# Zero matmuls ahead of five waits of TensorE in a fused attention, routing and expert kernel

## The chip, the cores and the metric

The kernel runs on one core of one Trainium2 chip. A core has five engines that run beside each other and meet through semaphores: TensorE (PE in the rows; PEld is its weight load) multiplies matrices into PSUM, VectorE (DVE) and ScalarE (ACT) work element by element, GpSimd (POOL) does the same more slowly and issues gathers and scatters, and SyncE (SP) issues most of the transfers. PSUM has eight banks here, of 128 partitions by 2 KB. The metric is the device time of one execution in microseconds (us), the median of several runs.

## The reference, cut to what matters

```python
for t in range(S):                      # 2 batches, 8 heads, 768 steps, head size 40
    m_new = maximum(f[t] + m, i[t])
    f_stab, i_stab = exp(f[t] + m - m_new), exp(i[t] - m_new)
    C = f_stab * C + i_stab * outer(v[t], k[t]);  n = f_stab * n + i_stab * k[t]
    y[t] = sigmoid(o[t]) * (C @ q[t]) / maximum(abs(n @ q[t]), 1)
x = y.reshape(1536, 320)
noisy = x @ w_gate + log1p(exp(x @ w_noise)) * noise
# the 2 largest of 8 experts per row, softmax over the two
out = sum over the row's two experts of  weight * (relu(x @ w1[e]) @ w2[e])
# second layer: all 4 experts for every row, weighted by domain_probs
out2 = sum over e of p[:, e] * (relu(out @ v1[e]) @ v2[e])
```

## The kernel before, in words

The recurrence is computed in chunks of 128 time steps, 6 per batch, so 12 chunks i = 0 to 11 (0 to 5 are batch 0). For a chunk, `o_S(i, g)` (L338) multiplies keys and queries of four heads into a bank `sp`, for g = 0 and 1; `o_M` (L345) multiplies that by the decay mask `A` on VectorE; the mask comes from exponentials on ScalarE (`o_decay`, L327) and a triangle select on GpSimd. `o_U`, `o_Cg` and `o_Cu` carry the state `C` from chunk to chunk (GpSimd scales it by `gb`, VectorE adds the bank `up`). `o_inter` (L391) and `o_AV` (L402) fill the bank `hp`; ScalarE copies it to `hs`; `o_tp` turns it; `o_x` (L418) normalises and gates it on VectorE and so writes the chunk's rows of `x`. `o_xp` (L434) transposes these, `o_lp` and `o_lt` make the routing logits from them.

When chunks 0 to 3, then 0 to 5, have logits, `route(b, h)` (L478) ranks the experts on VectorE, counts ranks with ones-matmuls into the bank `pp` and computes a row number `slot` for each token. GpSimd then scatters the token numbers into the table `Td` in memory, eight scatters for h = 0 and four for h = 1, and `tok` is read back from it. With `tok`, GpSimd gathers the rows of the first expert unit (`xload`); `prep` transposes and splits them into a high and a low part (`xh`, `xl`), and `moe1(0)` (L638) begins with bank `s1`. From there on matmuls of the experts follow each other, with the rest of batch 1's attention and routing woven in. In parallel SyncE streams weights (`raw`), which ScalarE and VectorE split into a high and a low part (`w1hi`, `w1lo`, `w2hi`, `w2lo`).

What sets the order: the written order is that of the software pipeline `STEP` (L47), of the strings `PLAN1` and `PLAN2`, and of `weave`. On top of it the language's scheduler places the instructions of each engine by when it estimates their inputs ready, so that an instruction can stand behind others that were written after it. Each engine then executes its list strictly in that order, and waits where an input is missing. PSUM tiles take the eight banks in turn, in the order in which they are written in the program. At the start of the program there are already 11 matmuls of zeros (`WARM`).

Of the kernel before, what the change touches and what calls it, by code (L numbers as in the profile page):

```python
# [16 lines left out]
P = 128  # L17
# [15 lines left out]
LEAD = 6  # L33
PARTS = [slice(0, 1), slice(1, 2), slice(2, 4), slice(4, NC)]
WARM = 11
PLAN1 = "AAAAAAAAAAAzAAoAAAArrwArAwArrrrrArArrrrwrAAArrrArArrAwrrArArAArrrrArrrArA"
PLAN2 = "A AA  AA r A AAA r rr rr A  A AA Ar ArrrrrrrrrA Arr r  A rrrr   rr rrrrr rr  r Arr rArr r  r "
RAW = 3 * F // NQ
# [27 lines left out]
def body(ctx: ExitStack, tc: tile.TileContext, d, o, dbg=None):  # L66
    nc = tc.nc
# [10 lines left out]
    def psum(shape, name):  # L78
        uid[0] += 1
        return ps.tile(shape, F32, tag="ps", name=f"{name}_{uid[0]}")  # L80


    zero = at.tile([P, 4 * P], BF16, name="zero")
# [95 lines left out]
    def w_next(n, k, q):  # L179

        assert STREAM[pos[1]][1:] == (n, k, q)
        w_split()
        w_load()
# [5 lines left out]
    def stage1(out_ps, w1, f, xh, xl):  # L189
        hi, lo = weights[w1, 1, f // (NF // NQ)]  # L190
        c = slice((f % (NF // NQ)) * P, (f % (NF // NQ) + 1) * P)
        seq = [(hi[:, 0, c], xh[:, 0]), (hi[:, 0, c], xl[:, 0]), (hi[:, 1, c], xh[:, 1]), (hi[:, 1, c], xl[:, 1]), (lo[:, 0, c], xh[:, 0]), (lo[:, 1, c], xh[:, 1]), (hi[:, 2, c], xh[:, 2]), (lo[:, 2, c], xh[:, 2])]
        for i, (l, r) in enumerate(seq):
            nc.tensor.matmul(out_ps, l, r, start=(i == 0), stop=(i == len(seq) - 1))  # L194
# [15 lines left out]
    def relu_split(hh, hl, src):  # L210
        nc.scalar.activation(hh, src, AF.Relu)  # L211
        nc.vector.scalar_tensor_tensor(hl, src, 0.0, hh.bitcast(F32), ALU.max, ALU.subtract)  # L212
# [114 lines left out]
    def o_decay(i, g):  # L327
# [7 lines left out]
        nc.gpsimd.affine_select(A[:, hs_], A[:, hs_], pattern=[[0, 4], [1, P]], compare_op=ALU.is_ge, fill=0.0, base=0, channel_multiplier=-1)  # L335
        t["d", g] = last.ins

    def o_S(i, g):  # L338
        t = st[i]
        sp = psum([P, 4, P], "sp")  # L340
        for j in range(4):
            nc.tensor.matmul(sp[:, j, :], t["kp"][:, 4 * g + j, :], t["qt"][:, j, :], start=True, stop=True)  # L342
        t["sp", g] = sp
# [90 lines left out]
    def o_xp(i):  # L434
        b, c = divmod(i, NC)
        xp = psum([P, 3, P], "xp")
        for k in range(2):
            nc.tensor.transpose(xp[:, k, :], xs[b][:, c, k * P : (k + 1) * P], ident)
        nc.tensor.transpose(xp[0:DR, 2, :], xs[b][:, c, 2 * P : DM], ident)
        xt = at2.tile([P, 3, P], F32, name="xt")  # L440
        nc.scalar.copy(xt[:, 0:2], xp[:, 0:2])
        nc.vector.tensor_copy(xt[0:DR, 2], xp[0:DR, 2])
        st[i]["xt"] = xt
# [34 lines left out]
    def route(b, h):  # L478
# [7 lines left out]
        n = HALVES[h]  # L486
# [3 lines left out]
        sp = at.tile([P, HC, E1], F32, name=f"spl{h}")  # L490
# [15 lines left out]
        for k in range(2):  # L506
            nc.vector.tensor_scalar(sel[:, k, n], rk, float(k), None, ALU.is_equal)
        yield
        pp = psum([P, HC, E1], "pp")
        nc.tensor.matmul(pp, tri, selb[:, n], start=True, stop=False)  # L510
        last = c0 + HC - 1
        for i in range(1, last + 1):
            j = max(i, c0)
# [3 lines left out]
        g = at.tile([P, HC, E1], F32, name=f"g{h}")  # L517
# [67 lines left out]
    def tiles(n):  # L585

        return [P] * (CAP // P) if len(UNITS[n][1]) == 1 else [min(P, JCAP - i) for i in range(0, JCAP, P)]

    def xload(n):
        if n >= len(UNITS) or n in xes or n in preps or not routed.issuperset(UNITS[n][1]):  # L590
            return
        e, bs = UNITS[n]
        col = 0 if bs[0] == 0 else CAP // P
        first = n < ALONE
        X = (Xall[:NC] if first else Xall).rearrange("t p c -> (t p) c")
        xe = m1.tile([P, len(tiles(n)) if first else NCOL, DM], F32, name="xe")
        for s, r in enumerate(tiles(n)):
            nc.gpsimd.indirect_dma_start(out=xe[:r, s, :], out_offset=None, in_=X, in_offset=bass.IndirectOffsetOnAxis(ap=tok[bs[-1]][:r, e, col + s : col + s + 1], axis=0))
        xes[n] = xe

    def prep(n):
        if n >= len(UNITS):
            return
        xe = xes.pop(n)
        N = sum(tiles(n))
        pa = psum([P, 2, N], "pa") if 2 * N <= 512 else None
        pk = [pa[:, k] if pa is not None else psum([P, N], "pa") for k in range(2)]
        pb = psum([DR, N], "pb")
        for s, r in enumerate(tiles(n)):
            c = slice(s * P, s * P + r)  # L610
            for k in range(2):
                nc.tensor.transpose(pk[k][:, c], xe[:r, s, k * P : (k + 1) * P], ident[:r, :r])
            nc.tensor.transpose(pb[:, c], xe[:r, s, 2 * P :], ident[:r, :r])
        W = CAP if n < ALONE else JCAP
        xh = m1.tile([P, 3, W], F32R, name="xh")[:, :, :N]
        xl = m1.tile([P, 2, W], F32R, name="xl")[:, :, :N]
        if pa is not None:
            split(xh[:, 0:2], xl, pa)
        else:
            for k in range(2):  # L620
                split(xh[:, k], xl[:, k], pk[k])
        nc.scalar.copy(xh[0:DR, 2], pb)
        nc.vector.tensor_sub(xh[DR:P, 2], pb, xh[0:DR, 2].bitcast(F32))
        preps[n] = xh, xl
# [9 lines left out]
    def flush():  # L634
        while ystore:
            ystore.pop()()

    def moe1(n):  # L638

        e, bs = UNITS[n]  # L640
        w = wn[n]
        ahead = n + 1 == len(UNITS) or wn[n + 1] != w
        xh, xl = preps.pop(n)
        for j in (n + 1, n + 2):
            xload(j)
        ts = tiles(n)
        N = sum(ts)
        W = CAP if n < ALONE else JCAP
        hh, hl, both = [], [], []
        half = len(ts) - 1 if ts[-1] < P else None  # L650
        M = (N - ts[-1]) if half is not None else N
        for f in range(0, NF, 2):

            hf = m1.tile([P, 2, 2 * W], F32R, name="hh", bufs=5)
            hhf, hlf, htf = hf[:, :, :N], hf[:, :, 2 * N - M : 2 * N], hf[:, :, N : 2 * N - M]
            pair = psum([P, 2, N], "s1") if 2 * N <= 512 else None
            for i in range(2):
                hp = pair[:, i] if pair is not None else psum([P, N], "s1")
                stage1(hp, w, f + i, xh, xl)
                if pair is None:  # L660
                    nc.scalar.activation(hhf[:, i], hp, AF.Relu)
                    for l, c in ((hlf, slice(0, M)), (htf, slice(M, N))):
                        nc.vector.scalar_tensor_tensor(l[:, i], hp[:, c], 0.0, hhf[:, i, c].bitcast(F32), ALU.max, ALU.subtract)
                hh.append(hhf[:, i])
                hl.append(hlf[:, i])
                both.append(hf[:, i, M : 2 * N - M])
            if pair is not None:
                relu_split(hhf, hlf, pair)
            if f == 2:
                flush()  # L670
            if n == 0 or wn[n - 1] != w:
                w_next(w, 2, f // 2)
            yield
        if n + 1 in xes:
            prep(n + 1)
        yps = [psum([P, DM], "s2") for _ in ts]
        for q in range(NQ):
            stage2(yps, w, hh, hl, q, half=half, both=both)
            if ahead:
                w_next(w + 1, 1, q)  # L680
            if q < NQ - 1:
                yield
        ys = m1.tile([P, len(ts) if n < ALONE else NCOL, DM], F32, name="ys", bufs=2 if n < ALONE else 1)
        for s, r in enumerate(ts):
            if r == P:
                nc.vector.tensor_copy(ys[:, s], yps[s])
            else:
                nc.scalar.copy(ys[:r, s], yps[s][r:])
                nc.vector.tensor_add(ys[:r, s], yps[s][:r], ys[:r, s])
        row = first_row(e, bs[0])  # L690

        def store():
            k = sum(r == P for r in ts)
            nc.sync.dma_start(Yd[row : row + k * P].rearrange("(s p) c -> p s c", p=P), ys[:, :k])
            if k < len(ts):
                nc.sync.dma_start(Yd[row + k * P : row + N], ys[: ts[k], k])

        ystore.append(store)
        if n in (len(UNITS) - 1, LAST0):
            flush()  # L700
        yield
# [145 lines left out]
    def og_load(b):  # L847
        nc.sync.dma_start(xs[b], d["og"][b])

    if WARM:  # L850
        wps = psum([P, 4 * P], "warm")
        for i in range(WARM):
            nc.tensor.matmul(wps, zero[:, :P], zero, start=(i == 0), stop=(i == WARM - 1))
    og_load(0)
# [69 lines left out]
    W0 = splits()  # L924
    for w in PLAN1:
        if w in "zo":
# [123 lines left out]
```

## Time and profile before

| | us |
|---|---|
| median of 3 runs | 710.69 |
| lowest and highest | 710.33, 712.83 |
| the profiled execution | 708.15 |
| its span, first to last instruction | 706.1 |
| TensorE busy in the span | 680.1 (96%) |
| VectorE, ScalarE, GpSimd busy | 369.3, 262.1, 126.1 |
| mean granted clock of TensorE | 0.976 |

Times inside the program are counted from the start of the span. The profiled execution is 2.05 us longer than its span and 2.54 us shorter than the median. [...] A square bracket at the end of a row of the timeline is the time for which the engine stood idle before that group, and what ended it. Busy times of a matmul group run to a modelled end and overlap the next group's start.

### The profile page before, as it was taken

How to read it: one execution, taken by the hardware profiler on the slowest of the kernel's cores; microseconds unless marked ns; L12 is line 12 of the kernel's file. 1: busy time of each engine (PE TensorE's matmuls, PEld its weight loads, DVE VectorE, ACT ScalarE, POOL GpSimd, SP SyncE). 2: the span in 40 equal slices, each digit the busy share in tenths (PEclk: the TensorE clock that was granted, in tenths of full speed). 3: DMA queues.
4: the chain of work that ended last, by engine and by line, in shares of the span. 5: the costliest groups of instructions: out<-in, count | busy, mean ns of one | idle time of the engine just before them, and what ended most of it. 6: DMA issues, size and time to landing. Idle time of an engine off the chain costs nothing.

```text
span 706.1 us, 11386 instructions
## 1 busy us (share of the span) xinstructions
PE 680.1 (96%) x4427; PEld 622.7 (88%) x4427; DVE 369.3 (52%) x787; ACT 262.1 (37%) x501; POOL 126.1 (18%) x183
## 2 busy tenths in 40 slices
PE   9898688999999999999999999999999999999997
PEld 6776577999899999999889899898898998989987
DVE  7868587877565664658756334412444224332141
ACT  5558446763453543545541223302233113121120
POOL 5544572142612101124023000000000000000000
PEclk9998779999999999999999999999999999999999
DMA  6889647665665444567662003100130001001011
GB/s 195 220 246 302 196 115 234 194 202 168 172 195 163 136 135 148 135 189 244 187 189 75 1 19 109 38 1 1 31 103 31 1 1 37 1 1 39 1 37 41
DMA packets 39946, 80.03 MB, mean 113 GB/s; under 512 B 9377, under 2 KB 16465, under 8 KB 39889
## 3 DMA queue, kind: packets, MB, share of 16 engines
q1 hardware_dynamic: 36496, 70.39, 33.2%
q0 software_dynamic: 3392, 8.86, 4.5%
q8 instruction: 37, 0.61, 0.4%
q14 instruction: 21, 0.16, 0.1%
HBM read 70.20 MB, written 9.04 MB: 112 GB/s over the span
## 4 chain that ended last, share of the span: by engine, by line
PE 79%; DMA 10%; DVE 5%; issue 2%; ACT 1%; POOL 1%; SPq 0%; ACTq 0%; DVEq 0%; POOLq 0%
PE z L194 25%; PE z L208 24%; PE s L194 12%; PE s L208 10%; DMA raw<-w 4%; DMA A<-LFd 2%; PE sp L342 1%; PE s L204 1%; DMA raw<-v 1%; DMA Td<-toki,slot 1%; DMA kp<-kT 1%; DVE w2lo L175 1%; PE lp L449 1%; PE hp L407 1%; POOL Td L540 1%
## 5 line engine op out<-in xcount | busy, mean ns | idle before, releaser
L211 ACT ACTIVATE hh<-z 128x512 fp32r<-128x512 f32 x96 | 57.1, 600 | 192.4 <-PE z L194 192.3
L208 PE MATMUL z<-w2hi,hh 128*128 128x320 f32 x384 | 118.6, 309 | 0.0
L208 PE MATMUL z<-w2hi,hl 128*128 128x320 f32 x384 | 118.3, 308 | 0.0
L208 PE MATMUL z<-w2lo,hh 128*128 128x320 f32 x384 | 118.3, 308 | 0.0
L194 PE MATMUL z<-x2h,w1hi 128*128 128x512 f32 x288 | 112.4, 390 | 0.0
L208 PE MATMUL s<-w2hi,hh 128*128 128x320 f32 x448 | 107.6, 312 | 1.7 <-ACT hh L211 0.9
L212 DVE SCALAR_TENSOR_TENSOR hl<-z,hh 128x512 fp32r<-128x512 f32 x96 | 65.8, 690 | 82.5 <-ACT hh L211 82.5
L194 PE MATMUL z<-x2h,w1lo 128*128 128x512 f32 x288 | 96.6, 389 | 0.0
L194 PE MATMUL s<-xh,w1hi 128*128 128x256 f32 (+1 forms) x288 | 84.5, 312 | 3.3 <-ACT xh L186 3.3
L175 DVE TENSOR_TENSOR w2lo<-raw,w2hi 128x640 fp32r<-128x640 f32 x60 | 49.6, 828 | 65.6 <-ACT w2hi L174 65.5
L208 PEld LDWEIGHTS s<-w2hi,hh 128*128 128x128 f32 x448 | 76.7, 188 | 2.8 <-ACT hh L211 1.2
L174 ACT CAST w2hi<-raw 128x640 fp32r<-128x640 f32 x60 | 43.5, 728 | 87.2 <-PE s L204 25.3
L194 PE MATMUL z<-x2l,w1hi 128*128 128x512 f32 x192 | 74.8, 390 | 0.0
L175 DVE TENSOR_TENSOR w1lo<-raw,w1hi 128x768 fp32r<-128x768 f32 x60 | 57.2, 957 | 29.8 <-ACT w1hi L174 29.2
L208 PEld LDWEIGHTS z<-w2lo,hh 128*128 128x128 f32 x384 | 72.1, 188 | 0.6
L208 PEld LDWEIGHTS z<-w2hi,hh 128*128 128x128 f32 x384 | 72.1, 188 | 0.5
L208 PEld LDWEIGHTS z<-w2hi,hl 128*128 128x128 f32 x384 | 72.1, 188 | 0.0
L194 PE MATMUL s<-xh,w1lo 128*128 128x256 f32 (+1 forms) x288 | 70.5, 309 | 0.0
L208 PE MATMUL s<-w2lo,hh 128*128 128x320 f32 x224 | 69.2, 309 | 0.0
L194 PEld LDWEIGHTS z<-x2h,w1lo 128*128 128x128 f32 x288 | 54.1, 188 | 11.3
L174 ACT CAST w1hi<-raw 128x768 fp32r<-128x768 f32 x60 | 49.9, 836 | 36.7 <-PE s L194 15.3
L194 PEld LDWEIGHTS z<-x2h,w1hi 128*128 128x128 f32 x288 | 54.0, 188 | 10.8
(188 smaller groups left out, 1025.0 us busy)
## 6 DMA issues: line engine op xcount, KB each, us to landing
raw<-w SPq DMA_DIRECT2D x44, 384.0 KB
raw<-w SPq DMA_DIRECT2D x44, 320.0 KB
raw<-v SPq DMA_DIRECT2D x16, 384.0 KB
A<-LFd SPq DMA_DIRECT2D x10, 512.0 KB
raw<-v SPq DMA_DIRECT2D x16, 320.0 KB
kv<-kv SPq DMA_DIRECT2D x12, 324.0 KB
Yd<-ys SPq DMA_DIRECT2D x8, 320.0 KB
qt<-qT SPq DMA_DIRECT2D x12, 208.0 KB
```

Of the source, the lines that this page charges most:

```text
L174: nc.scalar.copy(hi, raw)
L175: nc.vector.tensor_sub(lo, raw, hi.bitcast(F32))
L194: nc.tensor.matmul(out_ps, l, r, start=(i == 0), stop=(i == len(seq) - 1))
L204: nc.tensor.matmul(yp, both[f], r[:, k], start=(f == 0 and i == 0), stop=(f == NF - 1 and i == 1))
L208: nc.tensor.matmul(yp, l, r, start=(f == 0 and i == 0), stop=(f == NF - 1 and i == 2))
L211: nc.scalar.activation(hh, src, AF.Relu)
L212: nc.vector.scalar_tensor_tensor(hl, src, 0.0, hh.bitcast(F32), ALU.max, ALU.subtract)
L342: nc.tensor.matmul(sp[:, j, :], t["kp"][:, 4 * g + j, :], t["qt"][:, j, :], start=True, stop=True)
L407: nc.tensor.matmul(hp[64 * j : 64 * j + 41, p, :], t["kv"][:, 4 * j + p, D:], t["A"][:, 4 * j + p, :], start=False, stop=(p == 3))
L449: nc.tensor.matmul(lp[32 * k : 32 * k + 32], wgn[r, k, :], st[i]["xt"][r, k, :], start=True, stop=True)
L540: s = nc.gpsimd.indirect_dma_start(out=Td, out_offset=bass.IndirectOffsetOnAxis(ap=slot[b][:, k, c : c + 1], axis=0), in_=toki[:, b * NC + ...
```

## The change

Five places get matmuls of a zero tile, written ahead of the instructions that would wait, into the same bank, which those instructions begin anew with `start=True`. So the values in the bank are not changed by them. The zero tile exists already. The places are the scores of chunk 7 and of chunk 9 (g = 0), the transposes `xp` of chunks 6 and 7, the rank count of `route(0, 1)` and the first bank of `moe1(0)`. Of these the rank count gets a bank of its own, `fl`, so every later PSUM tile takes the next bank in turn. In all there are 8 + 3 + 8 + 18 + 5 + 8 = 50 matmuls: 24 of 512 columns and 26 of 384.

```diff
+FILL_S = {(7, 0): 8, (9, 0): 3}
+FILL_X = {6: 8, 7: 18}
...
+    def fill(out, n):
+        for _ in range(n):
+            nc.tensor.matmul(out, zero[:, :P], zero[:, : out.shape[-1]], start=True, stop=True)
...
         sp = psum([P, 4, P], "sp")
+        if (i, g) in FILL_S:
+            fill(sp.rearrange("p j l -> p (j l)"), FILL_S[i, g])
...
         xp = psum([P, 3, P], "xp")
+        if i in FILL_X:
+            fill(xp.rearrange("p k l -> p (k l)"), FILL_X[i])
...
+        if (b, h) == (0, 1):
+            fill(psum([P, 4 * P], "fl"), 5)
         pp = psum([P, HC, E1], "pp")
...
             pair = psum([P, 2, N], "s1") if 2 * N <= 512 else None
+            if n == f == 0:
+                fill(pair.rearrange("p i c -> p (i c)"), 8)
```

The scheduler counts the new matmuls as work of TensorE, and so the order around them moves on every engine. On TensorE, before, around the scores of chunk 7 (`sp_915` is g = 0, `sp_1000` g = 1; `up_896` and `hp_977` belong to chunk 6, `lp_920` to chunk 4, `tp_955` and `xp_1005` to chunk 5):

```order
L376 MATMUL up_896<-kv,kw 40x41 x8
L342 MATMUL sp_915<-qt,kp_164 128x128 x4
L449 MATMUL lp_920<-xt,wgn 32x128 x3
...
L415 MATMUL tp_955<-ident,hs 128x105 x4
...
L342 MATMUL sp_1000<-qt,kp_164 128x128 x4
L407 MATMUL hp_977<-A,kv 41x128 x8
L438 MATMUL xp_1005<-ident,x_85 128x128 x2
```

and in the changed kernel (`sp_915` again g = 0 and now `sp_1008` g = 1, `hp_985` chunk 6, `xp_1013` chunk 5):

```order
L386 MATMUL up_896<-kv,kw 40x41 x8
...
L344 MATMUL sp_915<-zero 128x512
...
L461 MATMUL lp_928<-xt,wgn 32x128 x3
...
L425 MATMUL tp_963<-ident,hs 128x105 x4
...
L417 MATMUL hp_985<-A,kv 41x128 x8
L352 MATMUL sp_915<-qt,kp_164 128x128 x4
L352 MATMUL sp_1008<-qt,kp_164 128x128 x4
L450 MATMUL xp_1013<-ident,x_85 128x128 x2
```

The zeros stand where the scores stood, and the scores themselves have moved behind the logits of chunk 4, the rank count, and the last products of chunk 6. On ScalarE, before, from the sigmoid of batch 1's gate (`x_86`) on:

```order
L272 ACTIVATE x_86<-x_86 128x1920
L451 COPY ls<-lp_920 96x128
L333 ACT_TABLE_LOAD
L333 ACTIVATE A<-A,as_t 128x128 x8
L441 COPY xt<-xp_1005 128x256
L409 COPY hs<-hp_977 105x512
L174 CAST w1hi<-raw 128x768 x3
```

and in the changed kernel:

```order
L463 COPY ls<-lp_928 96x128
L275 ACT_TABLE_LOAD
L275 ACTIVATE x_86<-x_86 128x1920
L453 COPY xt<-xp_1013 128x256
L419 COPY hs<-hp_985 105x512
L336 ACT_TABLE_LOAD
L336 ACTIVATE A<-A,as_t 128x128 x8
L177 CAST w1hi<-raw 128x768 x3
```

The eight exponentials of the masks have moved behind the copy of `xp` of chunk 5 and that of `hp` of chunk 6. On GpSimd, before, around the eight scatters of `route(0, 0)`:

```order
L335 AFFINE_SELECT A<-A 128x512
L353 TENSOR_TENSOR qg<-qt,gb 104x512
L335 AFFINE_SELECT A<-A 128x512
L540 DMA Td<-toki,slot_89 10240x1 x8
L335 AFFINE_SELECT A<-A 128x512
L368 TENSOR_TENSOR C_190<-C_188,gb 40x4x41 x2
```

and in the changed kernel:

```order
L554 DMA Td<-toki,slot_89 10240x1 x6
L338 AFFINE_SELECT A<-A 128x512
L554 DMA Td<-toki,slot_89 10240x1 x2
L338 AFFINE_SELECT A<-A 128x512
L363 TENSOR_TENSOR qg<-qt,gb 104x512
L338 AFFINE_SELECT A<-A 128x512
L378 TENSOR_TENSOR C_190<-C_188,gb 40x4x41 x2
```

Two selects and the product `qg` have moved from ahead of the scatters to between and behind them. In both kernels the second of the two instructions on `C_190` waits, besides for VectorE, for the landing of all eight scatters.

## Rows read from the trace of the kernel before

**Rows 1.** Windows by stage: busy time of each engine (instructions), granted clock, DMA share, GB/s.
```profile
58.40:65.30 6.90, 6.90 (x38) 5.46 (x40) 5.96 (x28) 5.70 (x12) 1.16 (x3) 0.51 1.02 285
65.30:75.50 10.20, 7.41 (x87) 5.77 (x83) 9.56 (x27) 8.10 (x20) 7.85 (x8) 1.00 0.97 273
75.50:85.80 10.30, 9.04 (x61) 7.72 (x63) 3.29 (x16) 2.58 (x4) 4.03 (x6) 0.50 0.70 218
...
89.60:99.40 9.80, 8.91 (x57) 7.43 (x58) 7.93 (x29) 5.00 (x15) 6.77 (x9) 0.50 0.38 89
...
114.10:706.10 592.00, 584.31 (x3591) 545.69 (x3591) 285.32 (x542) 200.44 (x340) 63.16 (x62) 1.00 0.31 93
```
**Rows 2.** Timeline, TensorE's five waits: start, duration, engine, line, operation, idle before it.
```profile
58.36 1.93 PE L342 MATMUL sp<-qt,kp 104*128 104x128 f32 x8 [2.34 <-DMA A<-LFd]
...
73.64 0.41 PE L438 MATMUL xp<-ident,x 128*128 128x128 f32 x2 [1.96 <-DVE x L428]
...
76.76 0.20 PE L510 MATMUL pp<-selb,tri 128*128 128x16 bf16 x1 [1.59 <-DVE selb L505]
...
90.48 0.66 PE L438 MATMUL xp<-ident,x 128*128 128x128 f32 x2 [4.07 <-DVE sf L535]
...
114.13 0.50 PE L194 MATMUL s<-xh,w1hi 128*128 128x256 f32 x2 [2.69 <-ACT xh L186]
```
**Rows 3.** Timeline, TensorE, one round of chunks at either clock.
```profile
92.84 2.08 PE L342 MATMUL sp<-qt,kp 104*128 104x128 f32 x8
...
100.38 0.44 PE L438 MATMUL xp<-ident,x 128*128 128x128 f32 x2
...
102.17 1.16 PE L342 MATMUL sp<-qt,kp 104*128 104x128 f32 x8
...
106.23 0.38 PE L438 MATMUL xp<-ident,x 128*128 128x128 f32 x2
...
110.59 0.85 PE L407 MATMUL hp<-A,kv 128*41 128x128 f32 x10
```
**Rows 4.** Timeline, TensorE, the start of the program.
```profile
1.39 4.88 PE L853 MATMUL warm<-zero 128*128 128x512 bf16 x11 [1.39 <-POOL zero L84]
...
10.43 3.78 PE L342 MATMUL sp<-qt,kp 104*128 104x128 f32 x16
```
**Rows 5.** The chain that ended last: start, duration, engine or transfer.
```profile
61.31 6.10 DMA kp<-kT
...
77.63 7.52 DMA Td<-toki,slot
...
106.58 6.15 DMA raw<-w
```
**Rows 6.** Timeline, ScalarE, masks and casts.
```profile
61.74 1.28 ACT L333 ACT_TABLE_LOAD   x1
63.04 2.44 ACT L333 ACTIVATE A<-A,as_t 128x128 f32<-128x128 f32 x8
66.57 0.37 ACT L441 COPY xt<-xp 128x256 f32<-128x256 f32 x1 [1.09 <-PE xp L439]
...
67.32 2.31 ACT L174 CAST w1hi<-raw 128x768 fp32r<-128x768 f32 x3
```
**Rows 7.** Timeline, VectorE, routing and output of a chunk.
```profile
60.15 0.18 DVE L505 TENSOR_SCALAR selb<-rk 128x32 bf16<-128x32 f32 x1
...
67.55 0.15 DVE L536 CAST slot<-sf 128x8 int32<-128x8 f32 x1
...
89.40 0.94 DVE L428 TENSOR_TENSOR x<-xo,rd 128x320 f32<-128x320 f32 x1
...
90.36 0.68 DVE L348 TENSOR_TENSOR A<-sp,A 128x512 f32<-128x512 f32 x1
...
91.02 0.48 DVE L360 TENSOR_TENSOR kw<-kv,w_t 128x320 f32<-128x320 f32 x1
```
**Rows 8.** Timeline, GpSimd, the first scatter.
```profile
68.00 1.22 POOL L540 DMA_INDIRECT Td<-toki,slot  x1 [0.83 <-DVE xt L442]
```

## The prediction

> **What bounds the kernel now.** I read the windows by stage first. From 114.1 us on TensorE is busy 584.31 of 592.00 us at full clock [rows 1]; there only its own work counts, and the change takes nothing from it. So what can be won lies before 114.1, in how early the experts' matmuls begin. There three stages ran at half clock: 58.4 to 65.3, 75.5 to 85.8 and 89.6 to 99.4, with 6.90, 9.04 and 8.91 us of busy TensorE [rows 1]. Each follows one of the waits of the timeline, of 2.34, 1.96 and 1.59, and 4.07 us; a fifth of 2.69 us stands before the experts [rows 2]. Half clock nearly doubles the work: one group of scores took 2.08 us at 92.84 and 1.16 at 102.17 [rows 3]. At full clock the three stages would hold 12.4 us less work of TensorE.
>
> The chain of waits, read next, says how much of that is on the path. In the first stage the path is a transfer of keys (6.10 us from 61.31); its scores could not start before 67.41 at any clock. In the second it is the landing of the last of eight scatters, 7.52 us from 77.63 to 85.15, for which GpSimd's second product on `C` waits; VectorE stands behind it, and with it the output `x` of chunk 7, which ends at 90.34 [rows 5, 7]. TensorE's 9.04 cold us lie beside that transfer and cost nothing. Only in the third stage is TensorE itself the path, from `xp` of chunk 7 at 90.48 to `xp` of chunk 8 at 100.38 [rows 2, 3]. So of 12.4 us about a third can be had.
>
> **The change part by part.** *Price of the zeros.* 11 matmuls of 512 columns took 4.88 us at the start, 0.444 each, and the scores behind them took 3.78 us for two groups, so 1.89 for one, nearer to 2.08 than to 1.16 [rows 3, 4]. Halved, a zero matmul of 512 columns costs 0.22 at full clock, one of 384 columns 0.17. The six groups then take 1.8, 1.3, 1.1, 0.7, 3.0 and 1.8 us in the order in which TensorE meets them, 9.7 in all; at half clock 19.4. Where they stand in a wait they are free: 1.8 of 2.34, 1.3 of 1.96, 1.1 of 1.59, 3.0 of 4.07, 1.8 of 2.69 [rows 2]. The group of three has no wait of its own (0.7 us), but stands in the second stage, beside the scatters.
>
> *First stage.* The zeros end at 57.8 instead of a wait to 58.36. The rank count still can't start before `selb` is ready at 60.33 [rows 7]. The moved scores of chunk 7 then end at about 64.7 at full clock, and `xp` of chunk 5 behind them at 65.2, some 1 us earlier than before. But the exponentials, which ran from 63.04 to 65.48 [rows 6], now stand behind that `xp`: 65.2 plus the two copies (0.75 from 66.57 to 67.32), the table load (1.28) and 2.44 put their end at 69.7 and the end of the three casts (2.31) at 72.0, where it was 69.63 [rows 6]. VectorE needs the casts before it makes `x` of chunk 6, which comes about 2.4 us later. This loss lies beside the scatters as well, as long as `x` of chunk 6 and the next rank count are done before they land; I take it as nothing, and as up to 2.4 us if that cover goes.
>
> *Scatters.* On VectorE `slot` no longer stands behind two half-clock rounds of scores and a `kw`; I put it at 66.0 instead of 67.70, and the first scatter at 66.2 instead of 68.0 [rows 7, 8]. From 68.00 to 77.63 eight issues are 1.38 apart [rows 5, 8]; with the select of 0.65 now between them the last is issued at 66.2 + 7 x 1.38 + 0.65 = 76.5, 1.1 us earlier. If it lands 7.5 us later, as before, `x` of chunk 7 waits for 84.0 instead of 85.15. In front of it there now stand, however, one mask product (0.68), one `kw` (0.48) and some three small operations of the size of `selb` (0.18), 1.6 us, so that it ends 0.5 us later than before. That is the upper bound. The lower: SyncE's loads behind chunk 7's `hp` are issued later, the scatters meet less traffic and land at 81 to 81.5; then VectorE's own queue decides, and `x` of chunk 7 ends 2.3 us earlier. The nearest row is neither; I take the middle, 0.9 us earlier.
>
> *Third stage.* From `xp` of chunk 7 to that of chunk 8 took 100.38 - 90.48 = 9.90 us cold; the next round of the same work took 106.23 - 100.38 = 5.85 at full clock [rows 3]. In the new order VectorE has more to do before `xt` of chunk 7, which I count as one wait of 1.0 us of TensorE. Saved: 9.90 - 6.85 = 3.1 us.
>
> *Up to the experts.* The next rounds ran at full clock already. The experts wait for `xh`, which waited for a weight transfer of 6.15 us issued at 106.58 behind the store of chunk 9 [rows 5]; now a different tile of that stream stands in that place, behind the same store, so the distance stays. The last eight zeros fit in that wait. But five of the eight (ten in the records) last products of chunk 11, 0.85 us, lay in this wait [rows 3] and now follow the first expert matmuls: 0.8 us more in the stage that TensorE bounds.
>
> Sum: 0.9 + 3.1 - 0.8 = 3.2 us less. The profiled execution of 708.15 (span 706.1 and 2.05 around it) becomes 704.95. The median of the runs is 710.69, 2.54 above that execution; the same difference gives 707.5, which I predict.
>
> *Where the clock is weighed.* Rows 4 leave open whether zeros move the clock: 4.88 us of them were not followed by full-speed scores. [...]
>
> **The rivals.** (a) The zeros do not hold the clock, and the change is slower. Then TensorE falls to half clock at 58.4 as before, the zeros behind it cost 2.7, 2.2, 1.3 and 6.0 us, and the moved scores are late by 2.2 us with all of ScalarE's queue. The place that decides is the 18 zeros: at full clock they end at about 88.5, ahead of `x` of chunk 7 at 89.4; in the cold case each of the groups in front of them ends later, and from the point where they end after `x`, every us is on the path. I work out 99 to 100 instead of 90.5 for `xp` of chunk 7 if nothing brings the clock back, less 3 us of warm third stage: 6 us slower. If the real scores bring it back midway, as they did at 85.8 [rows 1], 2 to 3 us slower. Middle: 4 us slower, 714.5. For it: rows 4. Against it: clock changes after gaps, not after full stretches, in rows 1.
>
> (b) The clock holds, but TensorE was hidden: the scatters land as late as before, VectorE's longer queue ends `x` of chunk 7 at the upper bound, and in the third stage VectorE, busy 7.93 of 9.80 us [rows 1], takes over as the bound, so that only 1.5 to 2 us of 9.9 go; with the 0.8 of the moved products and 0.5 this leaves 0.5 us: 710.2. For it: VectorE's share. Against it: part of its time there is waiting for cold matmuls.
>
> (c) The clock falls in a gap without zeros. In the new order there is one of about 1.7 us before the scores of chunk 8, whose keys land at 67.41 [rows 5], and one of about 1.8 us before `lt` of chunk 5, behind the late casts. A fall there makes the zeros before `xp` of chunk 6 and the rank count cold, 2.4 us more, on top of the late casts; part of it is covered by the scatters. About 1 us is left of the gain: 709.7.
>
> (d) The lower bound holds and the later stages lose their small waits too: 2.3 + 3.1 + 0.6 - 0.8 = 5.2 us, 705.5, and down to 703.
>
> **How the numbers follow.** Forecast (706.3 to 708.9) 0.34; d 0.23; b 0.18; c 0.12; a 0.13. The range reaches from d's far end to most of c and b and a part of a: 703.2 to 712.3. A measurement of this kernel can tell about 0.5% from no change, 3.55 us here. The forecast lies just on the near side of that: 0.2 of its 0.34 counts as faster with all of d, the rest with b and c as no change, and a as slower except for its mildest case: faster 0.43, same 0.45, slower 0.12.
>
> **What would show it.** Right: granted clock 1.00 from 58 us on in all windows; `xp` of chunk 7 at 89 to 90 and `xp` of chunk 8 less than 7 us later; the first expert matmul at 110 to 111.5 instead of 114.13; `C` of chunk 8 still waiting for a scatter's landing. Wrong: windows at 0.50 behind a group of zeros (a or c); `xp` of chunk 7 directly behind the 18th zero (a); TensorE idle for several us in the third stage at full clock (b); or the casts of the first weights, rather than the scatters, ahead of `x` of chunk 7 in the chain.

## The result: slower by about 1%, and the profile after

| | before | after |
|---|---|---|
| median of four runs each | 710.68 us | 717.75 us |
| lowest and highest | 710.33, 712.83 | 715.86, 718.96 |
| the profiled execution, its span | 708.15, 706.1 us | 717.14, 715.3 us |

The ratio is 1.010, interval 1.007 to 1.013. Two later comparisons of the same kernel, with more runs, gave 1.0068 (1.0036 to 1.0100) and 1.0085 (1.0050 to 1.0119). So the change costs 5 to 7 us, where 3.2 us of gain were predicted. Single executions of before spread from 699.0 to 716.4 us over the chips used here; below, verdicts rest on ratios, and a profile shows where time lies in one execution.

First the windows of the changed kernel over the stages of [rows 1] (busy time of TensorE, its loads, VectorE, ScalarE, GpSimd; granted clock as a share of full speed; DMA share; GB/s):

```profile
58.40:65.30 6.90, 5.13 (x63) 4.11 (x63) 6.39 (x32) 4.03 (x5) 0.20 (x1) 1.00 1.02 286
65.30:75.50 10.20, 6.68 (x33) 5.72 (x34) 4.18 (x10) 8.74 (x22) 7.83 (x7) 0.69 0.95 276
75.50:85.80 10.30, 7.99 (x66) 5.22 (x66) 9.48 (x27) 4.71 (x9) 7.52 (x9) 0.83 0.67 201
89.60:99.40 9.80, 9.80 (x92) 7.43 (x91) 8.06 (x30) 4.05 (x12) 7.61 (x9) 1.00 0.35 92
```

The third stage ran at clock 1.00 instead of 0.50, as the change wanted. Whether the zeros did it, these windows alone don't show; that is taken up below. The clock fell in other places: the second of these windows stood at 1.00 before and stands at 0.69 now. TensorE's timeline, with the rows that answer to [rows 2 and 3], shows after which gaps, and where the zeros lie (L344 is the matmul of zeros):

```profile
60.30 0.19 PE L524 MATMUL pp<-selb,tri 128*128 128x32 bf16 x1 [1.42 <-DVE selb L517]
...
68.82 1.74 PE L352 MATMUL sp<-qt,kp 104*128 104x128 f32 x8 [3.80 <-issue]
...
77.60 0.44 PE L450 MATMUL xp<-ident,x 128*128 128x128 f32 x2
...
82.47 0.18 PE L524 MATMUL pp<-selb,tri 128*128 128x16 bf16 x1 [2.13 <-DVE selb L517]
...
90.50 3.09 PE L344 MATMUL xp<-zero 128*128 128x384 bf16 x18
93.43 0.38 PE L450 MATMUL xp<-ident,x 128*128 128x128 f32 x2
...
99.52 0.41 PE L450 MATMUL xp<-ident,x 128*128 128x128 f32 x2
...
111.64 0.63 PE L344 MATMUL s<-zero 128*128 128x512 bf16 x1
112.49 1.98 PE L344 MATMUL s<-zero 128*128 128x512 bf16 x6 [0.22 <-issue]
114.12 0.47 PE L197 MATMUL s<-xh,w1hi 128*128 128x256 f32 x1
```

The transposes of chunk 7 stand directly behind the 18th zero, at 93.43 instead of 90.48; those of chunk 8 follow 6.09 us later instead of 9.90. The first expert matmul starts at 114.12, before at 114.13. So in these two executions nothing is won or lost up to there, and all of the 9.2 us of span come behind it. Windows of before, then of after: from the first expert matmul to the results of the fourth unit, from there to those of the fifth (the first of batch 1), and to the end.

```profile
114.10:179.20 65.10, 65.07 (x506) 63.23 (x507) 51.02 (x138) 37.59 (x62) 17.32 (x17) 1.00 0.64 185
179.20:198.40 19.20, 17.98 (x134) 16.74 (x134) 12.56 (x19) 9.77 (x16) 10.68 (x12) 1.00 0.66 191
198.40:706.10 507.70, 501.26 (x2955) 465.72 (x2954) 221.74 (x387) 153.09 (x262) 35.16 (x34) 1.00 0.26 78
```

```profile
114.10:182.10 68.00, 66.29 (x518) 63.99 (x517) 48.36 (x136) 35.54 (x59) 16.53 (x17) 1.00 0.58 170
182.10:205.60 23.50, 21.07 (x136) 19.58 (x135) 12.01 (x18) 9.64 (x16) 11.27 (x12) 0.85 0.57 159
205.60:715.30 509.70, 502.75 (x2953) 466.99 (x2951) 221.80 (x387) 153.60 (x262) 35.26 (x34) 1.00 0.26 78
```

I call the first the early experts' stretch. It grew by 2.9 us: 1.2 us more work of TensorE and 1.7 us of idle TensorE. The second grew by 4.3 us, at clock 0.85. The third grew by 2.0 us.

A cause of 0.91 us of the 1.7 us of idle time shows on ScalarE, in the copy `xt` of chunk 10. In before it came 0.9 us behind the first expert matmul (first fence). In after, the transposes that feed it stand at 118.14 on TensorE instead of 114.47, and the copy itself stands behind a cast that waits 1.37 us for a weight transfer (second fence); TensorE waits 0.91 us for it at 120.54 (third fence). The output of chunk 11 is late behind it (stored at 128.48 instead of 127.33), and with it batch 1's routing: its first scatter starts at 147.12 instead of 145.75, the gathers for the fifth unit at 179.64 instead of 175.74.

```profile
115.05 0.37 ACT L441 COPY xt<-xp 128x256 f32<-128x256 f32 x1
```

```profile
111.72 0.59 ACT L189 CAST xh<-pa 128x512 fp32r<-128x512 f32 x1 [0.63 <-PE pa L626]
...
119.00 0.73 ACT L177 CAST w2hi<-raw 128x640 fp32r<-128x640 f32 x1 [1.37 <-DMA raw<-w]
119.63 0.59 ACT L214 ACTIVATE hh<-s 128x512 fp32r<-128x512 f32 x1
120.12 0.36 ACT L453 COPY xt<-xp 128x256 f32<-128x256 f32 x1
```

```profile
120.54 0.41 PE L461 MATMUL lp<-xt,wgn 128*32 128x128 f32 x4 [0.91 <-ACT xt L453]
```

### The profile page after: what moved, and what is told of

Read it like the earlier page. It is cut to its first block, busy times and chain, and to the rows that moved or that the text cites. A ratio compares the mean times of both kernels' runs of the same rounds, so it can differ in the third digit from the quotient of the medians.

```text
span 715.3 us, 11487 instructions
## 1 busy us (share of the span) xinstructions
PE 689.5 (96%) x4474; PEld 628.2 (88%) x4477; DVE 367.0 (51%) x787; ACT 262.6 (37%) x501; POOL 126.6 (18%) x183
## 4 chain that ended last, share of the span: by engine, by line
PE 80%; DMA 6%; DVE 5%; issue 4%; POOL 3%; ACT 2%; POOLq 0%; ACTq 0%; DVEq 0%; SPq 0%
PE z L197 24%; PE z L211 24%; PE s L197 11%; PE s L211 10%; PE sp L352 2%; POOL Td L554 2%; DMA A<-LFd 2%; PE s L207 1%; DMA raw<-v 1%; PE hp L417 1%; PE pa L626 1%; PE lb L327 1%; PE lp L461 1%; DMA gb<-gd 1%; PE hp L410 1%
## 5 line engine op out<-in xcount | busy, mean ns | idle before, releaser
L215 DVE SCALAR_TENSOR_TENSOR hl<-z,hh 128x512 fp32r<-128x512 f32 x96 | 65.9, 690 | 84.4 <-ACT hh L214 84.4
L197 PE MATMUL s<-xh,w1hi 128*128 128x256 f32 (+1 forms) x288 | 86.3, 317 | 1.1 <-issue 1.1
```

## The experiments

Theory A: the loss is the new order of instructions behind the first expert matmul. Theory B: it is the zeros themselves, where they outlast their wait. Theory C: it is chance, by where the clock falls. Theory D came later: the new order around GpSimd's select in the attention. Each kernel was timed in five rounds (12 runs; e12 6) beside 23 to 35 of before on the same chip.

A scheduler sets the order, so an edit of the zeros moves other work too. Where an order is "held", this was added at the program's end, with a list `ORDER` of places in the traced program for each engine; it makes each instruction follow its predecessor on its engine without any wait:

```diff
+            seq = []
+            for r in runs.split():
+                a, _, z = r.partition("-")
+                seq += FILLS.get(r, []) if r[0] == "z" else own[int(a) : int(z or a) + 1]
+            for p, i in zip(seq, seq[1:]):
+                tc.add_manual_dep(i, p.name, mybir.DependencyInfo(mybir.DependencyClass.NoSync, ...
```

**e1 and e2: the last group taken away, and alone.** Order free.

```diff
# e1: of the changed kernel
-            if n == f == 0:
-                fill(pair.rearrange("p i c -> p (i c)"), 8)
# e2: of the changed kernel
-FILL_S = {(7, 0): 8, (9, 0): 3}
-FILL_X = {6: 8, 7: 18}
+FILL_S = {}
+FILL_X = {}
-            fill(psum([P, 4 * P], "fl"), 5)
```

> All groups of zeros but the last one (the eight before the first expert matmul); the scheduler then places the rest by itself. Theory A (order): the loss comes from the order that the last group causes, which puts the end of chunk 11 and the softmax inputs of batch 1 behind the first expert matmuls; without it the first expert matmul starts at about 112.3 us and nothing is given back later: 708 to 711 us. Theory B (the zeros themselves lie on the path, 2.2 us of the 18 and 1.8 us of the last eight): only 1.8 us come back, 716 us. Theory C (the clock fell by chance at 183 and 356 us, worth some 5 us): between 711 and 718 us, with no tie to the edit, and half-clock windows behind 180 us again.

> Only the last group of zeros (eight before the first expert matmul), nothing in the attention. Theory A: nearly the whole loss: the end of chunk 11 moves behind the first expert matmuls, the first scatter of batch 1 starts 1 to 1.5 us later than at 145.75, the gathers for the fifth unit later than at 175.74, TensorE waits there: 714 to 718 us. Theory B: the eight zeros fit in the wait of 2.69 us, so 710.7 to 712 us. Theory C: as before, 710.7 us, unless the clock falls.

Measured: e1 1.0038 (1.0004 to 1.0073), e2 1.0011 (0.9977 to 1.0045). The last group alone (e2) does not carry the whole loss; whether the others do (e1, up to 1.0073), these runs leave open. e1's stretch of the early experts was long all the same (68.3 us), although TensorE has the order of before there: ScalarE, VectorE and SyncE have not. So the last group is not the only one that moves that order.

**e3: all zeros in the old order.** `ORDER` is that of before.

> All 50 zeros, but every engine's instructions are held in the order that they had before the change, with each group of zeros directly ahead of the instruction whose bank it uses (on GpSimd one scatter of eight is issued ahead of a select instead of behind it). Theory A: no loss after 114 us, since the order there is the old one, and the third stage at full clock: 706 to 711 us. Theory B: the zeros cost what they cost in the changed kernel, 713 to 716 us. Theory C: 711 to 718 us with half-clock windows in the same places.

Measured: 1.0017 (0.9986 to 1.0048). Fifty zeros cost little or nothing where they don't move other work (by the interval at most 3.4 us): against B as the whole account.

**e4, e6, e7, e12, e17: the new order held, the number of zeros changed.**

```diff
-FILL_X = {6: 8, 7: 18}
+FILL_X = {6: 8, 7: 4}     # e4, e6, e17; e12: 36; e7: 18
-                fill(pair.rearrange("p i c -> p (i c)"), 8, "zm")
+                fill(pair.rearrange("p i c -> p (i c)"), 1, "zm")     # e4, e7
```

> The changed kernel's order of instructions on every engine, held, but the 18 zeros before the transpose of chunk 7 cut to 4 and the last eight cut to 1. Theory A: the order alone makes the loss, so most of it stays: the transposes of chunk 7 start at 91.3 instead of 93.6 us and the first expert matmul at 110.5 to 112.5, but batch 1's routing is still late by its place behind the experts' first matmuls: 714 to 717 us. Theory B: 3 to 4 us come back: 713 to 714.5 us, and the scatters of batch 1 are earlier by the same 3 to 4 us. Theory C: 711 to 718 us, decided by whether the clock falls behind 180 us.

> The changed kernel's order on every engine, held; only the 18 zeros before the transpose of chunk 7 are cut to 4. Theory B: the 2.2 us by which the 18 outlast the output x of chunk 7 come back, 2 us less than the changed kernel. Theory A (order) and its follower, that a weight transfer sets when the experts start: the transposes are 2 us earlier but the first expert matmul, or the wait behind it, takes it back: 0 to 1 us less than the changed kernel.

> The changed kernel's order on every engine, held; only the last eight zeros are cut to one. Theory B: the first expert matmul starts at 112.3 instead of 114.1 us, behind its own xh, and the end is 1.5 to 1.8 us earlier. Theory A: it starts 1.8 us earlier and then waits as much longer for the copy of chunk 10's transposes, which stands on ScalarE behind a cast that waits for a weight transfer: 0 to 0.5 us less than the changed kernel.

> The changed kernel's order on every engine, held, with 36 instead of 18 zeros before the transposes of chunk 7. Theory B (there they lie on the path, each 0.163 us): 18 more cost 2.9 us, the transposes start at 96.5 to 99 us, and the ratio to before rises from 1.007 to 1.010 to 1.012. If a wait for weights behind them had room left, less: 1.007 to 1.009. If each us there costs more than itself, as the 3.4 us for 14 zeros (2.3 us) suggest: 1.012 to 1.014.

> The changed kernel's order on every engine, held, with 4 instead of 18 zeros before the transposes of chunk 7, again. If the 14 zeros cost 2 us or more on the path: ratio to before 1.001 to 1.004, as in the first measurement. If that was luck and the order makes the loss alone: 1.005 to 1.009.

Measured: e4 1.0033 (1.0000 to 1.0065), e6 1.0016 (0.9979 to 1.0053), e7 1.0076 (1.0042 to 1.0109), e12 1.0112 (1.0055 to 1.0168), e17 1.0053 (1.0015 to 1.0090). No cost of the last eight shows (e7), although in the changed kernel's profile they ended 1.8 us after `xh`. The 18 cost something in this order: the three kernels with 4 have a mean of 1.0034, the three with 18 (e7 and the two of the changed kernel) 1.0076, some 3 us apart, with about 2 us of uncertainty either way. The 36 of e12 come out 2.5 us above the three with 18, less than its interval is wide. The profile of e4 shows how a gain ahead of the experts is taken back. Its first expert matmul started 4 us earlier than in before; then TensorE waited 2.56 us for the same copy `xt`, and ScalarE 3.03 us for the same weights (rows of TensorE, then of ScalarE):

```profile
110.06 0.39 PE L206 MATMUL s<-xh,w1hi 128*128 128x256 f32 x1 [0.41 <-ACT xh L198]
...
118.65 0.41 PE L471 MATMUL lp<-xt,wgn 128*32 128x128 f32 x4 [2.56 <-ACT xt L463]
```

```profile
117.11 0.72 ACT L186 CAST w2hi<-raw 128x640 fp32r<-128x640 f32 x1 [3.03 <-DMA raw<-w]
```

**e5 and e16: the changed kernel again.** No edit.

> The changed kernel itself, beside the kernel before on the same chip, in more runs than the first comparison. If the first comparison (four runs of each) measured the change, the ratio is 1.007 to 1.013 again. If its gap was in part luck of a few runs (Theory C: single executions of before have since spread from 699.8 to 711.9 us), the ratio lies at 1.002 to 1.006, by the side of the four variants measured so far.

> The changed kernel once more, beside the three above on the same chip, so that they can be compared with it directly: 1.005 to 1.010 if the two comparisons so far hold.

Measured: 1.0068 and 1.0085, as given above. The loss is real, and chance (C) is a part of the first 1.010 at most.

**e8, e11, e18: the old order held, zeros for the third stage alone.**

```diff
-FILL_S = {(7, 0): 8, (9, 0): 3}
-FILL_X = {6: 8, 7: 18}
+FILL_S = {(9, 0): 3}
+FILL_X = {7: 18}     # e11, e18: {7: 8}
-            fill(psum([P, 4 * P], "fl"), 5, "zfl")
-                fill(pair.rearrange("p i c -> p (i c)"), 8, "zm")
```

> The order of before on every engine, held, with only the two groups of zeros ahead of the third stage (3 before the scores of chunk 9, 18 before the transposes of chunk 7). The prediction's term: the third stage runs at full clock, 3.1 us less between the transposes of chunks 7 and 8, and the end 2 to 3 us earlier, ratio 0.996. The follower of Theory A: the third stage is as much shorter, but the weight transfer behind the store of chunk 9 or the gathers take most of it before the first expert matmul: 0 to 1 us earlier, ratio 0.999 to 1.001.

> The order of before on every engine, held, with 3 zeros before the scores of chunk 9 and 8 instead of 18 before the transposes of chunk 7, so that they end before x of chunk 7. If the 18 outlasting x cost 1.3 us in the run with 3 and 18 in the old order (transposes at 88.7 us, x ready at 87.4), that comes back: ratio 0.997 to 0.999. If a weight transfer takes back whatever is won before the experts, the ratio stays at 0.999 to 1.002.

> The order of before on every engine, held, with 3 zeros before the scores of chunk 9 and 8 before the transposes of chunk 7, again. If the third stage at full clock reaches the end: 0.995 to 0.998. If the wait for the fifth unit's gathers takes it back, as the first profile of this kernel suggests: 0.998 to 1.001.

Measured: e8 0.9996 (0.9960 to 1.0031), e11 0.9983 (0.9946 to 1.0020), e18 0.9981 (0.9949 to 1.0013). Even without any new order the gain that the prediction wanted comes out at 0.3 to 1.3 us, and with each interval reaching over 1 it isn't shown; e11 and e18, the same kernel, together give 1.3 us with some 1.7 us of uncertainty either way. In e11's profile the first expert matmul starts at 111.4, 2.7 us earlier than in before; the fifth unit's stretch then took 21.6 us instead of 19.2. In e18's profile it starts at 109.6, the two stretches behind it took 65.7 and 20.0 us, and the span was 701.8: there most of what was won stayed.

**e9 and e10: the first group alone, and all but the first.** Order free; `FILL_S = {(7, 0): 8}` and nothing else, and `FILL_S = {(9, 0): 3}` with the rest as in the changed kernel.

> Only the first group: eight zeros before the scores of chunk 7; the scheduler then places the rest, and as in the changed kernel the exponentials of chunk 8 and GpSimd's select of them stand later, the select behind six of the eight scatters. Theory D (the order around that select makes the output x of chunk 7 late): x of chunk 7 starts at 91 to 93 us instead of 89.4, the third stage stays cold, and the kernel is 1 to 4 us slower than before, ratio 1.002 to 1.006. Theory B (only zeros that outlast a wait cost): the eight fit in their wait, ratio 0.998 to 1.001.

> All groups but the first one; the scheduler then leaves the select of chunk 8 ahead of the scatters, as before the change. Theory D: x of chunk 7 starts at 87 to 89.5 us again, the scatters' landing decides, and the kernel is 2 to 5 us faster than the changed one: ratio to before 0.998 to 1.002. Theory B: the 18 zeros still outlast x of chunk 7, by 1 to 3 us, and the ratio stays at 1.004 to 1.008.

Measured: e9 1.0032 (0.9994 to 1.0070), e10 1.0068 (1.0031 to 1.0104). D as the whole account falls: without the first group (e10) the selects stand ahead of the scatters again, and the loss is whole. That they cost a part in the changed kernel is not excluded (e9). From the first expert matmul on, e10 has the order of the changed kernel on every engine and e9 that of before, so this pair fits A, though their intervals overlap. In e10's profile the 18 zeros do not even outlast `x` of chunk 7, so B does not explain it there:

```profile
86.45 3.09 PE L344 MATMUL xp<-zero 128*128 128x384 bf16 x18
...
91.89 0.44 PE L450 MATMUL xp<-ident,x 128*128 128x128 f32 x2 [2.35 <-DVE x L438]
...
92.80 2.08 PE L352 MATMUL sp<-qt,kp 104*128 104x128 f32 x8
```

**e13, e14, e15: either half of the new order.** `ORDER` is put together from the two orders. On TensorE the cut is at the first expert matmul, on VectorE just ahead of it, on ScalarE and SyncE at the transposes of chunk 9; GpSimd's order differs ahead of the cut alone.

```diff
# e13: new order ahead of the cut, old behind it, all 50 zeros; e15: with FILL_X = {6: 8, 7: 4}
# e14: old order ahead of the cut, new behind it, and one zero only, at the first expert matmul
-FILL_S = {(7, 0): 8, (9, 0): 3}
-FILL_X = {6: 8, 7: 18}
+FILL_S = {}
+FILL_X = {}
-            fill(psum([P, 4 * P], "fl"), 5, "zfl")
```

> All 50 zeros and the changed kernel's order in the attention, held; but from the first expert matmul on (on SyncE and ScalarE from the transposes of chunk 9 on) every engine has the order of before. Theory A (the order behind the first expert matmul makes most of the loss, 2 to 3 us between the first expert matmul and the results of the fourth unit): that stretch takes 65 to 66 us instead of 68, and the ratio falls from 1.007 to 1.001 to 1.004. Theory B (the zeros and the order in the attention make it): the stretch may shorten, but the ratio stays at 1.005 to 1.008.

> No zeros but one, and the order of before in the attention; from the first expert matmul on (on SyncE and ScalarE from the transposes of chunk 9 on) every engine has the changed kernel's order. Theory A: the stretch from the first expert matmul to the results of the fourth unit takes 67.5 to 69 us, ratio 1.003 to 1.006, though there are no zeros. Theory B: ratio 0.999 to 1.002.

> As the run with the old order behind the first expert matmul, and the 18 zeros cut to 4: both suspected costs gone. If the two add, this is no slower than before, ratio 0.997 to 1.001. If the attention's new order by itself costs (output x of chunk 7 2 to 4 us later than in before), 1.002 to 1.004.

Measured, beside e16 (1.0085) on one chip: e13 1.0035 (1.0001 to 1.0068), e14 1.0046 (1.0007 to 1.0084), e15 1.0038 (1.0007 to 1.0068). The old order behind the cut takes 1.0085 - 1.0035 = 0.0050 away, 3.5 us of 707.15, with about 2.5 us of uncertainty either way; the new one there by itself, without the zeros, costs 0.0046, 3.3 us (0.5 to 5.9). A holds for that part, measured from both sides, though its size is known only roughly. The early experts' stretch in e13, e14 and e16:

```profile
112.30:177.40 65.10, 65.10 (x507) 63.26 (x507) 50.95 (x138) 37.52 (x62) 17.64 (x18) 1.00 0.64 191
```

```profile
109.60:177.70 68.10, 67.96 (x516) 66.01 (x517) 50.12 (x137) 36.91 (x62) 18.93 (x19) 0.96 0.62 176
```

```profile
115.50:182.20 66.70, 65.75 (x516) 63.83 (x517) 50.06 (x138) 36.83 (x62) 18.13 (x18) 1.00 0.62 180
```

It is 65.1 us with the old order, as in before to a tenth, and longer with the new: e16's stretch has 0.6 us more work and 0.95 idle. e14's is long for another reason: it has 0.1 us of idle time, but its first 5 us ran at half clock (one expert matmul took 0.41 us there and 0.28 us from 115.4 on), which fell behind a wait of 1.71 us at 108.26, ahead of the cut. So for e14 the ratio speaks for A, not this length. In all eight profiles with the old order there (before, e3, e8, e9, e11, e13, e15, e18) this stretch lies between 65.1 and 65.9 us, mean 65.5; in the ten with exactly the changed kernel's order there (after, e4 to e7, e10, e12, e14, e16, e17) between 66.6 and 71.5, mean 68.0. The sets do not overlap. (e1 and e2, whose order there is neither, have 68.3 and 67.8.) Counted from the first expert matmul, `xt` of chunk 10 begins after 0.9 to 1.2 us in the eight and after 6.0 to 8.2 in the ten, and the first scatter of batch 1 after 31.6 to 31.9 and after 33.0 to 38.0. In nine of the ten, all but e14, TensorE waits 0.5 to 2.8 us for that `xt`; in the eight no such wait shows. No run moves this copy alone, so what the rest of the new order adds is not known.

## Why the prediction was wrong

**The step that failed** is the first paragraph's "there only its own work counts, and the change takes nothing from it". The early experts' stretch was priced with the 0.8 us of moved products alone. That term was about right (0.6 to 1.2 us). What it left out is that the zeros' group ahead of the experts and those in the attention also gave ScalarE, VectorE and SyncE a new order there: `xt` of chunk 10 behind some thirty expert matmuls and behind casts that wait for weights, the routing of batch 1 behind it. By the ratios of e13, e14 and e16 the new order there costs 3.3 to 3.5 us, roughly half of the loss, where the prediction had nothing beyond the moved products. The rule of the prediction, to count what a moved instruction is queued behind, was applied to the attention and not past 114.1.

**The zeros and the clock.** That zeros hold the clock went into the sum as the author's estimate; [rows 4] left it open. The numbers of the third stage were right: clock 1.00, 18 zeros in 3.09 us (3.0 predicted), 6.09 us to the next transposes (6.85 predicted, 9.90 before). The reason was in part luck. TensorE was busy up to the zeros at 90.50 and `x` of chunk 7 ended at 91.24, so in this execution they stood in a wait of some 0.7 us and not of 4.07. e9 has no zeros there, had no wait either, and ran the stage at full clock (first fence). That the clock held behind zeros shows in other runs: in e12, 36 of them filled 6.01 us, and the transposes behind them took 0.38 us (second fence), as at full clock in [rows 3]; and with the old order held, e3 and e8, with 18, had a clock of 1.00 from these transposes to the next, where before had 0.55. So rival a's premise, that the zeros don't hold the clock, fell. It was not held where a gap followed them in e10: behind 18 zeros and 2.35 us of idle time, the next scores took 2.08 us.

```profile
92.99 0.44 PE L450 MATMUL xp<-ident,x 128*128 128x128 f32 x2
...
94.34 1.16 PE L352 MATMUL sp<-qt,kp 104*128 104x128 f32 x8
```

```profile
90.70 6.01 PE L353 MATMUL xp<-zero 128*128 128x384 bf16 x36
96.55 0.38 PE L460 MATMUL xp<-ident,x 128*128 128x128 f32 x2
```

The clock did fall in gaps without zeros, as rival c said, and in the first place that it named: behind 3.80 us of idle time (about 1.7 foreseen) before the scores of chunk 8, at 68.82. The second fall was not where it looked for one, but behind the 2.13 us ahead of the rank count at 82.47. The windows 65.3 to 75.5 and 75.5 to 85.8 stood at 0.69 and 0.83.

**The scatters.** The issue times were right: the first at 66.08 (66.2 predicted), the last at 76.93 (76.5). But `x` of chunk 7 ended at 91.24, not 0.9 us before 90.34. The cover named there was gone: I let the late exponentials lie beside the scatters, "as nothing, and as up to 2.4 us if that cover goes", counting the select between the scatters as 0.65 us of GpSimd and not asking who waits for it. Rows of GpSimd, then of VectorE:

```profile
73.84 0.96 POOL L554 DMA_INDIRECT Td<-toki,slot  x1 [0.30 <-issue]
74.86 0.64 POOL L338 TENSOR_SCALAR_AFFINE_SELECT A<-A 128x512 f32<-128x512 f32 x1
...
76.93 0.96 POOL L554 DMA_INDIRECT Td<-toki,slot  x1 [0.30 <-issue]
77.90 0.98 POOL L338 TENSOR_SCALAR_AFFINE_SELECT A<-A 128x512 f32<-128x512 f32 x1
...
80.68 1.00 POOL L378 TENSOR_TENSOR C<-C,gb 40x164 f32<-40x164 f32 x2
```

```profile
78.91 0.69 DVE L358 TENSOR_TENSOR A<-sp,A 128x512 f32<-128x512 f32 x1 [0.52 <-POOL A L338]
79.51 0.64 DVE L508 TENSOR_TENSOR spl<-spl,noise 128x16 f32<-128x16 f32 x1
...
82.18 0.23 DVE L517 TENSOR_SCALAR selb<-rk 128x16 bf16<-128x16 f32 x1
...
90.75 0.49 DVE L438 TENSOR_TENSOR x<-xo,rd 128x320 f32<-128x320 f32 x1
```

The second select stands behind the eighth scatter, the mask product behind the select, and the next rank count's `selb` behind the mask product: the rank count came at 82.47 instead of 76.76. TensorE's last scores ahead of the transposes then ended only at 90.5, the 18 zeros followed them, and outlasted `x` by 2.2 us. Rival a had this place right and its cause wrong. The landing itself no longer held anything: both products on `C` ran from 80.68 without a wait, so all eight scatters had landed by 81.2, where the last landed at 85.15 before. That was the premise of the prediction's lower bound, 81 to 81.5; its 2.3 us did not come, because the engines' own queues had become the path. That less traffic would bring the landing forward was the author's estimate and was not shown: the DMA share from 75.5 to 85.8 was 0.67 here and 0.70 before.

**Up to the experts.** In the terms of the sum, the 0.9 us of gain at chunk 7's transposes became 2.95 us of loss, and the 3.1 us of the third stage became 3.81. So chunk 8's transposes were won by 0.86 us, not 4.0, and the experts began where they had. That the distance stays (it was 13.75 us, then 14.60) was the right kind of caution; e4 and e11 show that what is won there can be taken back behind it, by the same weights (3.03 us in e4) or by the fifth unit's gathers (waits of 0.93 and 0.88 us in e11, 0.25 and 0.27 in before), and e18 that it need not be.

**The rest.** Beside the 3.3 to 3.5 us, about 2.5 us (e13 and e15, 1.0035 and 1.0038, intervals from just over 0 to 4.8 us) are left to the new order and the zeros in the attention. How they divide stays open: cutting the 18 helps in the new order (some 3 us), and with the old order behind the experts no effect of it shows (e15 against e13, with about 2.4 us of uncertainty either way), so whether the parts add is not known. The 4.3 us more that the fifth unit's stretch shows in the first pair of profiles are mostly not the change's: e16, the same kernel, took 19.6 us there, and e3, with the old order, 21.2, both below the 23.5. Over the eight profiles with the old order and the ten with the new, its means are 20.8 and 21.1 us, those of the rest behind it 507.2 and 508.1, with ranges that overlap.

```profile
182.20:201.80 19.60, 17.64 (x133) 16.58 (x132) 12.44 (x18) 9.75 (x16) 10.93 (x12) 1.00 0.64 188
```

```profile
179.00:200.20 21.20, 19.31 (x134) 17.85 (x133) 12.53 (x19) 9.75 (x16) 12.28 (x12) 0.92 0.60 177
```

The clock in that stretch was 1.00 in one execution of the changed kernel (e16) and 0.85 in another (the first).

## What to carry to other kernels

Filler instructions are seen by the scheduler: beside their own time, where they outlast their wait, their price is the order that they give to every engine, far behind the place where they stand. Here that order was roughly half of the loss, 3.3 to 3.5 us of 5 to 7. Test them with the old order held before judging them, and read the new order of every engine, weight casts and their transfers included, past the stage for which the filler is meant. Ask of a gain ahead of a stream of weights what the next wait for those weights leaves of it: in e4, 4 us won ahead of the experts met waits of 3.03 us for weights and 2.56 us for the copy behind them.

## What the runs showed that was not expected

- The clock held behind zeros alone: 36 of them filled 6.01 us in e12, and the transposes behind them still took 0.38 us.
- Small operations on VectorE took up to three and a half times as long while GpSimd worked on `A`, `qg` and `C` (77.90 to 81.68): from 79.51 to 81.29 `spl` took 0.64 us, `nl` 0.55 and `df` 0.52, while in before the same three took 0.18, 0.16 and 0.29 from 74.90 to 75.84. This held `selb` back by about 1 us; it was not tested by itself.
- Executions of one kernel differ by more than its first four suggest: four of before spanned 2.5 us, the 34 beside e13 to e16 16.9 us (699.03 to 715.92).
